# Crossed Horner products for chunks 2 on, shared PSUM banks and a new order, in a delta-rule attention and feed-forward kernel

## The chip, the cores and the metric

The kernel runs on one core of a Trainium2 chip. A core has TensorE (PE in the profile; PEld is its loading of weights), VectorE (DVE), ScalarE (ACT), GpSimd (POOL) and SyncE (SP), which here only issues DMAs. Each engine takes its instructions in the order of its own queue, and semaphores hold one engine until another is done. The metric is the device time of one execution in microseconds.

## The reference

The first part is a linear attention with the delta rule, for 4 batches of 8 heads, 768 positions and head size 48. The keys are normalized per position; `state` is a 48x48 matrix per head.

```python
for t in range(S):
    y[:, :, t] = np.einsum('bhd,bhde->bhe', q[:, :, t], state)
    v_old = np.einsum('bhde,bhd->bhe', state, kt)
    state = state + bt[:, :, :, None] * np.einsum('bhd,bhe->bhde', kt, vt - v_old)
```

The second part takes the 3072 tokens of 384 channels through `w_in` (384x2048), the tanh form of GELU, and `w_out` (2048x384). Inputs and outputs are float32; the kernel computes its matmuls in bf16.

## The kernel before, in words

**Chunks and pairs.** The positions are cut into 12 chunks of 64. The 32 heads make 16 pairs `p`; one head of a pair lies on partitions 0 to 63, the other on 64 to 127 (`HALF`). So an operand of a chunk is a tile of 128 partitions x 16 pairs, and one matmul works on one head with a quarter of TensorE's array.

**Work of a chunk.** `prep` and `prep2` normalize the keys and transpose them (`Kn`, `KQT`), `prepq` does so for the queries of two chunks. `gram` makes the key-key and query-key products, of which ScalarE stores the first (`G`) and VectorE the second, masked (`DT`). `blocks` inverts the triangular 16x16 blocks on the diagonal (`solve`, on GpSimd from chunk 1 on), and `back` transposes the result into `TB0` and `TB1`. `inverse` builds the inverse of the whole 64x64 triangle out of them: it expands the blocks into `WB` and `DI`, multiplies `G` by `WB` and masks it into `ET`, and then runs a Horner scheme over k = 1, 2, 3, in which each step multiplies the last result by `ET` and adds `DI`; the result is `TT`. `state` then makes the residual `R` (values minus what the state recalls), `U` = `TT` times `R`, the next state `S`, and the output of the chunk, which goes into `x`.

**The Horner steps.** Step k makes, for the columns from 16k on, a product of n = 64 - 16k columns (48, 32, 16) for each head: 32 matmuls in PSUM. For chunks 2 on, one VectorE instruction adds the matching columns of `DI` and writes `TT` in bf16. The first step reads `DI`, the others read what the step before has written to `TT`. For chunks 0 and 1 the sum is made in PSUM by matmuls with the identity, and the change does not touch them.

**Placement.** A matmul reads its operands from one half of the partitions and writes to one half of PSUM. In the straight placement, half a writes half a, so that only two of the four quarters of the array are ever used. In the crossed one, the even pairs do this, and the odd pairs write the other half, a ^ (p % 2), in the next bank, so that all four quarters are. Before the change, all of the other products of 32 matmuls of chunks 2 on are crossed (`fl`, in `prod`, `state`); the Horner products are straight. A product that is crossed twice comes out in its own half again, so `DI`, `TT` and `ET` of the odd pairs lie with swapped halves.

**Feed-forward.** `mlp(t)` works on a tile of tokens: chunks 0 to 3 make a tile each, and then two chunks make one. It computes 16 slices of `W1` times `x` in PSUM banks of 512 columns, ScalarE applies the GELU into `gT`, and `W2` times `gT` goes through `osb` to the output. These matmuls use the full array.

**Order.** Nothing is scheduled on the fly. Every operation is recorded by `op` (L101) with its readers and writers; the string `ORDER` (L18) then says which engine takes which operation and in what order, and `BANK` (L78) which PSUM bank each product gets. `w` items are filler matmuls on zeros (`spin`, L411) that keep TensorE busy. `BANKS` (L15) bounds the banks: "t", the attention, had 0 to 5, and "f", the feed-forward, 6 and 7, except for the last tile and early chunks ("l"). `schedule` (L136) gives an operation the waits of its inputs, and, where it takes a bank, those of the bank's earlier users. `load` (L480) issues the DMAs of keys, queries and values on SP, in order: a load behind one that waits for its buffer waits too.

**Lines of the profile.** Operations are recorded by helpers, so all matmuls but the transposes (L648, L680) and the fillers (L414) stand at L267, two-input VectorE and GpSimd operations at L251, copies of VectorE at L256, those of ScalarE at L260. Tile names tell them apart: ps<-DI,ET and ps<-TT,ET are the Horner products, TT<-ps,DI the additions, ps<-WB,G, ps<-R,TT, ps<-U,Kn and ps<-S,KQT crossed products, ps<-x,W and ps<-W,gT the feed-forward (m1 and W,gT below). L924, L931 and L915 expand the blocks.

Of the kernel before, what the change touches and what calls it, by code (L numbers as in the profile page):

```python
# [8 lines left out]
ALU = mybir.AluOpType  # L9
# [5 lines left out]
BANKS = {"t": (0, 6), "f": (6, 8), "l": (0, 8)}  # L15
# [3 lines left out]
v34 a50 g11 s49 v5 v0 g21 v46 a48 s47 g22 v6 g16 v8 v35 v41 g18 s54 v1 v4 a2 g13 g14 s55 g12 g19 v15 v45 s53 a26 v43  # L19
v33 v10 s56 v3 w6.7 p61 v36 v37 v9 v38 s51 v42 v7 v40 s52 a82 g84 v63 s60 a24 g20 v85 g17 a29 v39 v62 a30 a31 v83 a32  # L20
a23 v67 a86 s59 v70 a87 v64 v88 s57 a97 g75 v89 v65 g81 s58 w12.5 p91 v66 a98 p99 g90 v44 v92 g77 w1.4 p93 a103 v68
p100 v94 g72 g76 a101 s96 p152 v104 g74 v153 g73 a105 w1.7 p181 a106 a182 v107 v154 g108 v156 v155 g69 w8.3 p109 v157
v158 v159 a110 v160 v183 g80 s141 a102 v161 w4.5 p264 v162 v163 v164 p178 v265 a179 v165 g266 v166 a117 v167 v168 v169
v170 a25 a28 g267 a27 v171 g268 g269 v172 g270 g271 v173 g272 g273 v174 g274 g275 v175 g276 g277 v176 a185 g278 g279
s95 a184 v177 w29.3 p191 g280 p301 g281 v192 g282 a187 p189 v186 g283 v190 g284 a188 w1.5 p195 g285 v118 p193 g286
a196 g287 a194 p199 v71 g288 v180 p197 g289 a200 g78 a119 p203 v198 a120 g290 a205 p201 v121 g291 v204 v122 g79 a202
p209 a302 p206 g292 g293 s147 v207 a210 g294 g295 a125 v208 s140 v211 g296 w3.5 p215 v303 p216 g297 p217 s146 p304
v218 a219 p212 p123 v126 a305 g299 v298 a127 a128 v129 a133 v306 g130 v300 s115 v124 a213 s113 g400 w12.7 p131 v308
a309 s116 p398 v132 a311 s114 g603 v214 p399 a250 s111 p314 v401 a310 s112 a315 v251 s144 g402 s142 a375 v307 s143
g403 g404 w10.6 p312 v376 a135 s145 g405 p224 g406 s262 g407 p226 v377 a225 g408 v378 s263 v379 p328 a134 g409 v380  # L30
p228 v381 g410 v382 a313 s151 g411 v329 p136 g412 p137 s150 a229 g413 v383 p316 v138 p318 g414 s149 a317 v384 g415
p438 a227 v385 s223 p230 g416 v386 v139 a439 g417 s222 p232 a231 v387 g418 s148 v388 p320 a233 g419 v389 p459 v319
g390 s220 p234 a460 v440 s221 p322 a235 v321 p456 v461 p324 g420 a323 s396 a457 g393 p326 p441 s397 v327 a519 p236
v325 v458 p333 a442 g421 v520 p238 g422 a334 p391 g423 a253 v443 g424 p330 g425 a239 v331 p338 g426 p394 a252 v332
g427 v335 p339 v392 p340 g428 p341 a578 s259 p342 g429 p240 g430 v344 s260 g431 a343 g433 v579 a395 s258 p254 a237
g432 v580 p601 s345 v437 p602 s261 a444 v434 p241 s346 v462 s347 v604 p255 s348 a242 p349 s436 v256 g605 p351 a350
s435 v581 p644 v582 a352 p466 s531 v583 g521 p353 v584 a645 v585 s532 v445 p245 g522 a354 v646 a257 g606 v586 v587
g607 p355 g608 v464 a467 g609 p336 v588 v446 p448 g610 v337 p246 g611 a449 g612 v589 g613 v463 p523 g614 v590 a356
v591 p474 g615 v592 a247 p450 g690 a447 p357 v451 p359 v475 g593 p524 a360 p452 v525 a358 p468 g616 v453 a526 s599
p361 g596 v469 s600 p454 a362 p363 s527 v455 g617 v691 p476 s530 g618 p470 a477 g619 p480 s529 p594 g620 a364 p481  # L40
s528 g621 p478 a482 g622 p365 v479 s483 g623 a771 g624 s489 v471 p366 g625 s491 a595 v772 g626 s488 g627 g628 p533
a243 v773 s490 p662 v774 g629 p597 a244 v775 s492 g630 v776 p370 g631 a598 v777 s487 v778 g632 v779 g633 v780 s703
a367 g634 p371 v781 g636 v782 a692 s702 v783 v784 v785 g635 p794 v534 a372 a663 p795 v640 g786 a465 p493 v647 p495
v664 a494 g693 p472 v797 a496 p497 s792 g883 p499 v473 a498 s793 v637 p535 v648 s638 g796 p501 a536 v884 s699 p539
a502 p540 p641 g798 s486 v541 p694 a642 s639 p503 a500 v643 s700 g799 p695 a504 g800 p505 v696 g801 s548 p507 a506
s546 v697 p537 a665 s547 p651 g789 p659 v652 p509 s701 a508 s550 v538 a660 g802 p790 s549 g803 a374 p510 v661 g804
s698 a958 g805 v791 s551 g806 a249 v649 p837 g807 p669 v959 s484 p653 a248 g808 s485 p514 g809 a838 v654 g810 a668
g811 v670 a511 p515 g812 g813 v667 v839 g814 p552 g815 v960 a516 v961 p655 g816 v962 a553 p834 g817 v656 p677 a835
g818 p554 v963 g819 a650 v678 p556 g820 a555 g821 p657 v836 a557 g822 p558 v658 a886 g823 v666 g824 p679 g825 a559
p683 p671 g826 a680 g827 p560 g828 v672 p681 a561 p562 v682 g829 p673 a563 v830 p684 p704 v674 s832 a685 p564 v705  # L50
s545 p675 a565 s831 p852 v676 a369 p566 v964 s542 a853 v965 p710 v966 s544 p706 v967 a567 p568 v968 s543 v969 a707
v970 v841 a368 v854 p711 p855 v971 a712 p569 v860 v972 v859 g973 a856 v833 s719 p787 a373 v842 s720 p573 v857 a858
g885 s717 s721 p974 v840 a517 s722 p708 v788 p862 a570 g976 p574 s718 v863 a512 s688 v709 s687 g981 p864 a575 p977
s689 a576 v865 p887 s686 g1133 p888 v975 p723 v889 p844 a724 p725 v845 a861 p727 a843 v978 a726 p979 v890 a728 p980
p846 v982 p729 p731 v847 g983 a730 p1019 a732 p866 p1022 g984 v867 p848 g985 a1023 g986 p733 v849 g987 p735 g988 v1024
g989 p1131 a736 g990 g991 p1132 a734 g992 a1020 p737 g993 v1021 p739 g994 a738 g995 v1134 p870 a740 g996 p741 g997
p743 v871 a742 g998 g999 p850 a518 g1000 p868 a744 g1001 p745 v869 g1002 v851 p747 g1003 a746 g1004 p872 a748 p876
g1005 p749 a873 g1006 g1007 p751 a750 g1008 p874 g1009 a752 p877 g1010 v875 p753 a878 g1011 g1012 p1037 g1013 p891
a754 p755 v892 a577 g1135 a513 v1015 p897 a571 p893 s1016 g1014 p756 v894 a1038 s716 s715 g1136 v1018 g1137 p898 p1040
s714 g1138 a899 p759 g1139 s1017 v757 g1140 a1041 g1141 v1039 s713 p760 g1142 a572 v1043 s907 g1143 a1025 v1042 g1144  # L60
s906 p763 g1145 v1044 s904 v1026 g1146 a758 s908 g1147 v1045 v761 p1171 g1148 s905 p1029 a1172 p764 g1149 s909 a1028
g1150 v1173 s903 g1151 v1030 p767 g1152 a765 s881 g1153 v1027 s879 g1154 p1047 s882 g1155 p895 p1031 g1156 s902 p910
g1157 v1032 s880 g1158 p768 a911 g1159 v1048 g1160 g1161 p912 v896 g1162 g1163 p1174 g1164 a913 p1049 g1165 p1033 a769
v1050 a1175 p914 g1166 v1034 p916 a915 p1055 v1170 a917 p1051 p918 v1052 p920 v1177 a919 v1056 p1035 a921 p1053 a762
# [233 lines left out]
def bass_deltanet__then__act_gelu_tanh_kernel(  # L298
# [25 lines left out]
    with nc.allow_non_contiguous_dma("head rows"), nc.allow_low_precision("bf16 matmuls"):  # L324
# [568 lines left out]
        def inverse(c, hs):  # L893
# [5 lines left out]
            def nm(t, g):  # L899
                return [f"{t}_{y}" for y in ((g,) if c < 2 else (0, 1))]  # L900
# [439 lines left out]
```

## Time and profile before

| | us |
|---|---|
| runs | 252.25, 252.91, 249.76 (median 252.25) |
| profiled execution, span from first to last instruction | 249.4 |
| end of its last matmul | 246.5 |
| TensorE busy | 232.0 (93%) |
| VectorE busy | 161.4 (65%) |
| ScalarE busy | 139.0 (56%) |
| GpSimd busy | 118.6 (48%) |
| mean granted TensorE clock | 0.986 of full |
| 10 additions of 768 columns, mean | 0.945 |
| 10 of 512 columns | 0.686 |
| 10 of 256 columns | 0.421 |

The profiled execution's own time is not listed apart from the runs; its span is 0.4 us under the fastest of them and 2.85 us under the median. The busy time of an engine says little by itself, since the stages differ: up to about 43 us the chunk-0 chain runs through VectorE and TensorE is kept busy with fillers; from 50 us on TensorE has real work nearly always. The prediction therefore reads stages.

### The profile page before, as it was taken

What the parts mean: (1) busy time and instruction counts of PE and PEld (TensorE: products, weight loads), DVE (VectorE), ACT (ScalarE), POOL (GpSimd) and SP (SyncE); (2) the same over time, 40 slices, a digit from 0 to 9 for tenths busy, and PEclk for the clock granted to TensorE, in tenths of its full rate; (3) what the DMA queues carried; (4) which work ended last, traced back from release to release, by engine and by line L of the source; (5) the groups of instructions that cost most, each with busy time, mean ns of one, the idle gap of its engine ahead of it and who ended that gap; (6) DMA issues with size and microseconds to landing.
All of it is one profiled execution on the core that took longest, in us unless ns stands there. A gap on an engine that the chain in (4) does not pass through costs nothing.

```text
span 249.4 us, 12386 instructions
## 1 busy us (share of the span) xinstructions
PE 232.0 (93%) x5637; PEld 155.0 (62%) x5637; DVE 161.4 (65%) x316; ACT 139.0 (56%) x262; POOL 118.6 (48%) x249
## 2 busy tenths in 40 slices
PE   7577896998999799999899999999999999999995
PEld 4334473587778658868766655666656665555562
DVE  6699989886799399896969653767772465100001
ACT  2744578587686466838564357535682247426600
POOL 3685796688389858588045589883000000000000
PEclk9999999799999799999999999999999999999999
DMA  6999969996740825550244000623135210000112
GB/s 157 209 196 168 159 116 211 159 214 107 184 87 19 192 52 112 122 137 7 57 111 91 5 20 23 149 57 63 37 76 134 78 37 3 8 11 32 66 63 96
DMA packets 64789, 23.84 MB, mean 96 GB/s; under 512 B 53600, under 2 KB 63840, under 8 KB 64736
## 3 DMA queue, kind: packets, MB, share of 16 engines
q1 hardware_dynamic: 58656, 14.89, 30.8%
q0 software_dynamic: 1056, 3.15, 7.3%
q10 hardware_dynamic: 5024, 5.02, 6.3%
q8 instruction: 44, 0.72, 1.2%
q14 instruction: 9, 0.07, 0.1%
HBM read 20.64 MB, written 4.72 MB: 102 GB/s over the span
## 4 chain that ended last, share of the span: by engine, by line
PE 81%; DVE 10%; DMA 2%; issue 2%; ACT 2%; POOL 0%; ACTq 0%; POOLq 0%
PE ps L267 76%; DMA kf<-in_k_dram 2%; PE ps L648 2%; PE ps L680 2%; PE ps L414 1%; DVE ss L603 1%; DVE WB L931 1%; ACT WB L915 1%; DVE TB L806 1%; DVE KQT L256 1%; DVE ps L846 1%; DVE Yf L251 1%; DVE Tt L837 1%; DVE btz L251 0%; DVE ps L786 0%
## 5 line engine op out<-in xcount | busy, mean ns | idle before, releaser
L260 ACT ACTIVATE gT<-ps 128x512 bf16<-128x512 f32 x96 | 55.9, 597 | 38.4 <-PE ps L267 36.8
L267 PE MATMUL ps<-x,W 128*128 128x256 bf16 (+1 forms) x384 | 72.2, 329 | 0.0
L267 PE MATMUL ps<-W,gT 128*128 128x384 bf16 x384 | 67.0, 328 | 0.0
L267 PEld LDWEIGHTS ps<-W,gT 128*128 128x128 bf16 x384 | 36.4, 98 | 23.9 <-issue 0.5
L267 PEld LDWEIGHTS ps<-x,W 128*128 128x128 bf16 x384 | 39.1, 115 | 16.3 <-issue 0.3
L762 POOL TENSOR_TENSOR Yf<-Yf,tmp 128x28 f32<-128x28 f32 (+13 forms) x84 | 28.8, 342 | 6.4
L759 POOL TENSOR_TENSOR tmp<-Yf 128x28 f32<-128x28 f32 (+13 forms) x84 | 28.1, 335 | 6.1
L251 DVE TENSOR_TENSOR TT<-ps,DI 128x768 bf16<-128x768 f32 (+2 forms) x30 | 20.2, 684 | 13.8 <-PE ps L267 13.5
L414 PE MATMUL ps<-wz 128*128 128x512 bf16 x87 | 23.3, 416 | 1.4 <-DVE wz L409 1.4
L251 POOL TENSOR_TENSOR Kn<-kf,rn 128x768 bf16<-128x768 f32 (+1 forms) x11 | 16.0, 1452 | 17.1 <-DVE rn L629 10.1
L267 PE MATMUL ps<-KQT 48*32 48x32 bf16 (+1 forms) x1152 | 18.7, 195 | 5.8 <-issue 2.7
L260 ACT ACTIVATE osb<-ps 128x384 f32<-128x384 f32 x18 | 8.8, 490 | 26.3 <-PE ps L267 26.3
L256 DVE COPY osb<-ps 128x384 f32<-128x384 f32 x6 | 3.2, 552 | 29.8 <-PE ps L267 29.8
L260 ACT ACTIVATE G<-ps 128x512 bf16<-128x512 f32 x24 | 14.3, 597 | 11.4 <-PE ps L267 7.7
L267 PEld LDWEIGHTS ps<-KQT 48*32 48x32 bf16 (+1 forms) x1152 | 13.6, 95 | 10.9 <-issue 5.0
L719 DVE TENSOR_TENSOR DT<-ps,mD 128x512 bf16<-128x512 f32 x24 | 16.3, 680 | 4.1 <-ACT G L260 4.1
L267 PE MATMUL ps<-TT,ET 64*64 64x32 bf16 (+1 forms) x768 | 16.4, 176 | 0.0
L267 PEld LDWEIGHTS ps<-TT,ET 64*64 64x64 bf16 x768 | 14.8, 109 | 2.2 <-DVE R L251 0.6
L414 PEld LDWEIGHTS ps<-wz 128*128 128x128 bf16 x87 | 8.7, 105 | 11.5 <-issue 3.0
L251 DVE TENSOR_TENSOR S<-ps,S 128x768 bf16<-128x768 f32 x10 | 9.5, 953 | 9.0 <-PE ps L267 8.9
L260 ACT ACTIVATE x<-ps 128x1024 bf16<-128x1024 f32 (+2 forms) x10 | 9.2, 916 | 8.1 <-PE ps L267 7.9
L251 DVE TENSOR_TENSOR R<-ps,vf 128x768 bf16<-128x768 f32 x11 | 10.4, 949 | 3.8 <-PE ps L267 3.8
(122 smaller groups left out, 333.2 us busy)
## 6 DMA issues: line engine op xcount, KB each, us to landing
qf<-in_q_dram SPq DMA_DIRECT2D x24, 192.0 KB, 4.4
kf<-in_k_dram SPq DMA_DIRECT2D x23, 192.0 KB, 4.9
vf<-in_v_dram SPq DMA_DIRECT2D x40, 96.0 KB, 3.2
out_dram<-osb ACTq DMA_DIRECT2D x16, 192.0 KB, 2.0
W<-in_moe_w_out_dram POOLq DMA_DIRECT2D x4, 384.0 KB, 6.7
out_dram<-osb ACTq DMA_DIRECT2D x16, 96.0 KB, 2.8
W<-in_moe_w_in_dram POOLq DMA_DIRECT2D x4, 192.0 KB, 8.7
vf<-in_v_dram SPq DMA_DIRECT2D x4, 192.0 KB, 11.3
```

The lines of the kernel that those rows point to most:

```text
L251: return lambda e: e.tensor_tensor(out() if callable(out) else out, a() if callable(a) else a, b() if callable(b) else b, op)
L256: return lambda e: e.tensor_copy(out, a() if callable(a) else a)
L260: return lambda e: e.activation(out, a() if callable(a) else a, func)
L267: ins = t.matmul(out, lhsT, rhs, start=st, stop=sp_, skip_group_check=skip)
L414: ins = e.matmul(psum[:, b, :], wz[:, 0:128], wz[:, :], start=True, stop=True)
L603: op({"dve": 0.95 * w}, {"dve": lambda e, u=u: e.tensor_reduce(ss[j][:, u], sq[:, u, :], AX.X, ALU.add)}, reads=[f"sq{n}"], writes=[f"ss{j ...
L648: ins = e.transpose(o[:, a, j], Qn[:, n, a, j, :, :].rearrange("q h d -> q (h d)"), identB[:, :])
L680: ins = e.transpose(tb()[:, m, :], t[:, 2 * m:2 * m + 2, :].rearrange("p h d -> p (h d)"), identB[:, :])
L719: op(d_ps(512), {"dve": lambda e: e.tensor_tensor(dv, gview(1)(), md, ALU.mult)}, reads=[h] + MD, writes=[dn])
L759: sop(nb * s * w, lambda e, s=s, w=w, tv=tv: e.tensor_tensor(tv, yf[:, :, s:s + 1, 0:s].to_broadcast([128, nb, w, s]), Yv()[:, :, s + 1:16 ...
L762: sop(nb * s * w, lambda e, s=s, tv=tv: e.tensor_tensor(Yv()[:, :, s + 1:16, 0:s], Yv()[:, :, s + 1:16, 0:s], tv, ALU.add), [YN, TN], [YN])
L806: op({"dve": 0.58}, {"dve": lambda e: e.transpose(dst, src)}, reads=reads, writes=writes)
```

## The change

It has three parts. The Horner products of chunks 2 on are crossed: odd pairs write the other half of PSUM, in the second of two banks, and the addition, which has to bring them back to the half they belong to, becomes three VectorE instructions, one for the even pairs over all partitions and one for each half of the odd pairs. The bounds of the banks fall: all work may use all eight. And `ORDER` and `BANK` are new. Two operands of the product's record change with it: the bank class is "t", and the product takes two banks at every k.

In the new order the loads of the first keys, queries and chunk 0's values come as before; behind them the order differs. Fifty operations change their engine, most of them between VectorE and ScalarE: for instance the expansions of `WB` in chunk 1 go to ScalarE, and the `ET` products of chunk 1 to VectorE. VectorE's queue goes from 307 operations to 302, ScalarE's from 268 to 276, GpSimd's from 238 to 235, and TensorE has 88 fillers for 87. GpSimd issues the weights' loads in the same order. On SP, two of the four quarters of chunk 2's values now stand behind chunk 7's keys.

```diff
-BANKS = {"t": (0, 6), "f": (6, 8), "l": (0, 8)}
+BANKS = {"t": (0, 8), "f": (0, 8), "l": (0, 8)}
...
-                    op({"pe": 0.467 * w}, bk="l" if c < 2 else "t", fns={"pe": prod(hk, ET[e_], src[:, :, 16 * k - off:64 - off], n, per, g)},
-                       nm=int(32 * w), reads=nm(sn, y) + nm(f"ET{e_}", y) + ([f"DI{r_}e"] if fl else []), free=nm(f"TT{r_}b", y),
-                       writes=[hk], alloc=[(hk, max(1, int(NP * w) // per))])
-                    op(d_ps(16 * n * w), {"dve": f_tt(two(TT[r_][:, :, cols], per, g), view(hk, n, per, g),
-                                                      two(DI[r_][:, :, 16 * k - 16:48], per, g), ALU.add)},
+                    def place(p, hk=hk, n=n):
+                        return bank(hk, p % 2)[:, n * (p // 2):n * (p // 2) + n]
+
+                    def cross(src=src, off=off, k=k, place=place):
+                        return [(place(p)[HALF[a ^ (p % 2)], :], ET[e_][HALF[a], p, :], src[HALF[a], p, 16 * k - off:64 - off],
+                                 True, True, True) for p in range(NP) for a in range(2)]
+
+                    def add(e, hk=hk, n=n, k=k, cols=cols):
+                        for par, o_, i_ in ((0, slice(0, 128), slice(0, 128)), (1, HALF[0], HALF[1]), (1, HALF[1], HALF[0])):
+                            ins = e.tensor_tensor(TT[r_][o_, par::2, cols],
+                                                  bank(hk, par)[i_, 0:8 * n].rearrange("q (p t) -> q p t", t=n),
+                                                  DI[r_][o_, par::2, 16 * k - 16:48], ALU.add)
+                        return ins
+                    op({"pe": 0.274}, {"pe": f_mms(cross)}, bk="t", nm=32,
+                       reads=nm(sn, y) + nm(f"ET{e_}", y) + ([f"DI{r_}e"] if fl else []), free=nm(f"TT{r_}b", y),
+                       writes=[hk], alloc=[(hk, 2)])
+                    op({"dve": 3 * (0.10 + 1.06e-3 * 8 * n)}, {"dve": add},
                        reads=[hk] + nm(f"DI{r_}", y) + ([f"DI{r_}e"] if fl else []), writes=nm(f"TT{r_}b", y))
```

The lists of `ORDER` and `BANK` (about 1300 entries) are left out.

## The prediction

> **What bounds the kernel now.** I read the page's first two parts, the chain that ended last, a table by stages, and TensorE's timeline, in that order.
>
> The page: busy time of each engine, then the 40 slices.
>
> ```profile
> PE 232.0 (93%) x5637; PEld 155.0 (62%) x5637; DVE 161.4 (65%) x316; ACT 139.0 (56%) x262; POOL 118.6 (48%) x249
> ...
> PE   7577896998999799999899999999999999999995
> ...
> DVE  6699989886799399896969653767772465100001
> ...
> PE 81%; DVE 10%; DMA 2%; issue 2%; ACT 2%; POOL 0%; ACTq 0%; POOLq 0%
> ```
>
> TensorE is full from slice 8 (50 us) on, and the chain is 81% TensorE. VectorE is the second engine, and it is crowded only up to slice 33 (206 us); after that only the feed-forward part runs. In the chain in order of time, three pieces show where TensorE takes over:
>
> ```profile
> 39.90 2.58 DVE WB L931 x3
> ...
> 44.35 3.42 PE ps L414 x10
> ...
> 144.07 102.42 PE ps L267 x2080
> ```
>
> Up to 43 us the chain runs through VectorE; ten filler matmuls (L414) follow; the last 102 us are one unbroken stretch of matmuls. So past 50 us a microsecond of matmul is a microsecond of time, as long as the other engines keep up. The stage table shows how far they do (columns: stretch, length, then busy us of PE, PEld, DVE, ACT, POOL, then clock and DMA):
>
> ```profile
> 36.00:50.10 14.10, 12.00 (x304) 7.40 (x297) 12.82 (x26) 10.30 (x22) 9.38 (x16) 0.88 0.93 182
> 50.10:130.40 80.30, 77.01 (x2312) 61.05 (x2313) 64.78 (x128) 53.94 (x97) 54.09 (x104) 0.98 0.51 108
> 130.40:246.50 116.10, 115.42 (x2560) 70.74 (x2546) 53.46 (x77) 55.02 (x97) 30.62 (x69) 1.00 0.20 53
> ```
>
> I cut the stages where the first product of chunk 1's state ends (50.1 us) and where chunk 5's last state product ends (130.4 us). In the middle stage VectorE works 64.8 of 80.3 us, 15.5 us of slack; in the last, 53.5 of 116.1.
>
> **The product itself.** The edit turns the 30 Horner products of chunks 2 to 11 (10 chunks, k = 1, 2, 3) from the straight to the crossed placement. The other 64x64 products of these chunks are crossed already, so the timeline has both, 32 matmuls each (start, us, then what ran):
>
> ```profile
> 156.19 0.43 PE L267 MATMUL ps<-R,TT 64*64 64x48 bf16 x32
> 156.56 1.47 PE L267 MATMUL ps<-W,gT 128*128 128x384 bf16 x8
> ...
> 166.14 0.42 PE L267 MATMUL ps<-U,Kn 64*64 64x48 bf16 x32
> 166.40 0.69 PE L267 MATMUL ps<-DI,ET 64*64 64x48 bf16 x32
> 167.01 0.84 PE L267 MATMUL ps<-x,W 128*128 128x512 bf16 x3
> ...
> 169.98 0.66 PE L267 MATMUL ps<-DI,ET 64*64 64x48 bf16 x32
> 170.48 0.66 PE L267 MATMUL ps<-TT,ET 64*64 64x32 bf16 x32
> 171.07 1.49 PE L267 MATMUL ps<-x,W 128*128 128x512 bf16 x6
> ```
>
> From start to start, ahead of a full-array matmul: straight 0.61 (166.40 to 167.01), crossed 0.37 (156.19 to 156.56). Ahead of another 64x64 product: straight 0.50 (169.98 to 170.48), crossed 0.26 (166.14 to 166.40). The column count hardly matters (TT,ET of 32 columns is as long as DI,ET of 48). The difference is 0.24 either way. I take 0.21, since some neighbours shorten it by a few hundredths: 30 x 0.21 = **6.3 us less TensorE work**, bounds 5.4 (0.18) and 7.2 (0.24). The Trainium skill, "TensorEngine Tiling (Array Packing)", Theoretical Speedup, puts the gain of packing a small dimension at up to two times, which on the straight 0.50 to 0.61 would be 0.25 to 0.30 a product, 7.5 to 9 us; the rows say 0.24 and decide.
>
> **The additions.** Each of the 30 additions was one VectorE instruction; it becomes three (even pairs on 128 partitions, odd pairs as two half-height ones that cross the halves), each over half the columns. Rows by form: TT<-ps,DI of 768, 512 and 256 columns takes 945, 686 and 421 ns, 2.05 us a chunk. For the new sizes, 384 columns is ET<-ps,mE at 550, 256 is 421, 128 is the cast at 287. A half-height row costs what its columns say (bpad<-ps 64x192 takes 354), so height saves nothing. Three of each, with some 0.06 overlap between neighbours as in the timeline: 1.53 + 1.15 + 0.74 = 3.42 a chunk, 1.37 more; over ten chunks **+13.7 us on VectorE**. The strided write and the crossing of halves are in no row; bounds 1.0 to 2.0 us a chunk. It hides where TensorE has other work queued; where it has none, the next product waits for it, since k = 2 needs the sum of k = 1.
>
> **The new order** moves work too, and I counted it stage by stage. Between chunk 1's residual and chunk 5's state on VectorE it holds the twelve additions of chunks 2 to 5 (+5.5 us), two more ET products (+1.9) and two more long x copies for a short one (+1.8), and it loses KQT copies and a block expansion to ScalarE or to other stages (about -2.1): 64.8 + 7.1 = **72 us**. TensorE between the same two products loses 12 x 0.21 = 2.5 to the edit, and one m1 group (0.66), two W,gT groups (2.6) and two transposes (0.9) to other stages; two fillers come in (0.4). 77.0 - 6.3 = **71 us**, plus the 3.3 us in which it now idles there, 74. So the engines are level where VectorE had 15.5 us of slack. ScalarE gets eight operations more, some 5 us at the 597 ns of its commonest row, against 54 of 80 busy. All eight banks open to all work takes away waits for a bank; k = 2 and 3 now take two banks instead of one. No wait on a bank stands alone in the list of waits, so I set both at nothing, within 1 us either way.
>
> **Loads.** SP's queue is in order. In the new one two quarters of chunk 2's values stand behind chunk 7's keys, which wait until chunk 4's keys are read (Kn at 54.7 to 56.2 us now), and the second of them also behind a load of queries, the like of which is issued at 62.0 now. They land some 3.2 us after issue, by 66, and chunk 2's residual is due near 78: hidden by 12 us; beyond that, every microsecond counts. POOL's queue issues the same weight loads in nearly the old order. POOL's solves keep their rows; chunk 1's two XW products change places there, which brings the first 1.2 us later, to about 37.5, when VectorE comes to it near 38 anyway.
>
> **The start.** The DMA of chunk 0's keys and the chunk-0 chain stay. Then WB of chunk 1, the 2.58 us piece at 39.90, moves to ScalarE, where its three parts take 389 ns each, and chunk 3's transposed keys no longer stand behind it. Against that, two copies of chunk 0's factors (0.5 and 0.4) come onto VectorE, and chunk 0's x copy falls behind a table load (1.28 us). I take 1.5 us earlier into the middle stage; bounds 1 us later and 3 us earlier.
>
> **The end.** The last two copies to osb both fall on ScalarE, with output DMAs between them: +0.3 us.
>
> **The sum.** Middle stage: two engines with 74 and 72 us that feed each other with queues in order do not overlap perfectly; VectorE in its fullest stretch now (100 to 125 us) reaches 20.65 of 25, 83%. I take 77 (bounds 74, and 87.5 below): -3.3. Last stage: 3.8 us of feed-forward and transposes moved in, 18 x 0.21 = 3.8 out: level. Start -1.5, end +0.3: together -4.5. The profiled execution's span is 249.4, so 244.9. Its own time is not listed; the median of the runs shown, 252.25, lies 2.85 above the span, so **247.8 us** (-1.8%). The runs before differ by 1.2% among themselves; 2% is about what a measurement here can tell from no change.
>
> **Rivals.**
>
> 1. *VectorE is hidden.* The order interleaves feed-forward matmuls with nearly every Horner step, so TensorE might never wait. Middle stage 74 (-6.3), start -2, end +0.3: 241.4, a time of 244.2. For it: VectorE has no total overload. Against it: 72 of 74.
> 2. *VectorE becomes the bound and keeps its idle time.* Its 15.5 us of idle in the middle stage are mostly waits for a product ("TT <- ps" alone sums to 13.5 us over the run). The chain of one chunk (product, three instructions, product) gets longer, and S of chunk c gates R of chunk c+1. If all of it stays, the stage is 72 + 15.5 = 87.5 (+7.2); start level, end +0.3: 256.9, a time of 259.8, **slower**. It decides as soon as the stage passes 80.3 + 4.8, that is, if more than 13 us of the idle time stay; with less the time is within 2%. Against it: part of that idle came from TensorE being late, and TensorE has 6 us less to do. The Trainium skill, "TensorEngine Tiling (Array Packing)", PSUM Bottleneck, says that the copy out of PSUM may become the bottleneck once the array is packed, and asks for copies vectorized over tiles of a bank; the edit splits one instruction into three. By that rule this rival or the forecast holds, not the first.
> 3. *The crossed Horner products do not overlap* (each quarter waits for its sum): nothing off TensorE, additions still paid. Middle stage about 79.5, last +3.8, start -1.5, end +0.3: 251.2, a time of 254. WB,G and R,TT, crossed with the same shapes, speak against it.
>
> **Chances.** Forecast 0.37, VectorE hidden 0.28, VectorE bound 0.27, no overlap 0.05, something else 0.03. The forecast's own range is 245 to 251, a third of it under 247.2 (2% faster). Over all cases: faster by 2% 0.37 x 0.3 + 0.26 = 0.37 and a little; same 0.25 of the forecast, 0.08 of the second rival, 0.07 of the rest; slower mostly the second rival. I say 0.38, 0.40, 0.22. The range reaches from 1.7 under the first rival's time, for the upper bound of the product's gain, to most of the way to the second's: 242.5 to 256.
>
> **What would show it.** In the profile after: the products ps<-TT,ET and ps<-DI,ET of 32 should stand 0.26 to 0.37 from the next start; if 0.5, the third rival. TT<-ps,DI should appear as 90 rows with means near 550, 421 and 290 ns; means over 700 for the largest would make VectorE the bound. VectorE's busy share before chunk 5's state should pass 85%, and waits of PE or PEld for "TT L..." should grow from the 2.2 us they have now. If those waits stay under 2 us, the first rival holds; over 8 us, the second. The forecast is also wrong if TensorE's clock falls in new gaps (0.88 in the stage before 50 us now), or if the loads come late.

## The result and the profile after

The kernel after takes 249.76 us, the median of 20 runs (246.31 to 252.41, and one that stands alone at 525.61). The kernel before, in 20 runs beside it, takes 251.71 us (249.76 to 254.56). The ratio is 0.986, with an interval from 0.983 to 0.989: about 3.5 us faster. Ratios here leave out runs more than 1.5% above the fastest of their own kernel; the medians of all runs differ by less, 1.95 us or 0.8%. The profiled execution took 250.40 us, with a span of 248.6, and so lies in the upper half of its kernel; a second profile of the same kernel (after_again, below) has a span of 245.7.

The page after: busy time of each engine, the slices of TensorE and VectorE, the granted clock, and the chain that ended last.

```profile
PE 229.0 (92%) x5638; PEld 150.3 (60%) x5638; DVE 172.8 (69%) x368; ACT 139.7 (56%) x267; POOL 113.7 (46%) x246
...
PE   7587899999899898799999999999999999999995
...
DVE  6689957986878799799999576789887755100000
...
PEclk9999957999999999999999999999999999999999
...
PE 61%; DVE 24%; DMA 5%; SPq 4%; issue 3%; ACT 2%; POOL 0%; DVEq 0%
```

TensorE works 3.0 us less (232.0 before), VectorE 11.4 us more. The chain now runs through VectorE for 24% of the span, where it was 10%; in after_again, the same kernel, it is 13%. In the clock row, the sixth and seventh slice (31 to 43 us) stand at 5 and 7 tenths: that is the start of the kernel, and it comes back below.

The table by stages, cut at the same two products as before (stretch, length, busy us of PE, PEld, DVE, ACT, POOL, clock, DMA):

```profile
36.00:50.90 14.90, 14.23 (x350) 9.50 (x346) 12.70 (x25) 11.23 (x25) 9.91 (x17) 0.83 0.78 150
50.90:129.60 78.70, 72.55 (x2303) 55.65 (x2307) 68.49 (x150) 54.63 (x99) 50.26 (x101) 1.00 0.52 114
129.60:245.70 116.10, 114.69 (x2560) 68.80 (x2553) 63.69 (x116) 55.48 (x100) 30.09 (x69) 1.00 0.20 52
```

The middle stage begins 0.8 us later than before (50.9 against 50.1), is 1.6 us shorter (78.7 against 80.3), and the last stage is the same to 0.1 us. In the middle stage TensorE has 4.5 us less to do and idles 6.2 us where it idled 3.3. VectorE is busy 87% of that stage.

TensorE's timeline shows the products that were changed (start, us, what ran):

```profile
166.00 0.44 PE L266 MATMUL ps<-DI,ET 64*64 64x48 bf16 x32
166.28 0.40 PE L266 MATMUL ps<-KQT 48*64 48x128 bf16 x16
...
169.56 0.43 PE L266 MATMUL ps<-TT,ET 64*64 64x32 bf16 x32
169.83 0.42 PE L266 MATMUL ps<-DI,ET 64*64 64x48 bf16 x32
170.18 2.13 PE L266 MATMUL ps<-x,W 128*128 128x512 bf16 x9
```

From start to start they take 0.28, 0.27 and 0.35 us, where the straight ones took 0.50 and 0.61. The additions by form (busy us and mean ns of one, idle time of VectorE before them):

```profile
L1020 DVE TENSOR_TENSOR TT<-ps,DI 64x384 bf16<-64x384 f32 x20 | 11.1, 555 | 0.3
...
L1020 DVE TENSOR_TENSOR TT<-ps,DI 64x256 bf16<-64x256 f32 x20 | 8.4, 422 | 0.3
...
L1020 DVE TENSOR_TENSOR TT<-ps,DI 64x128 bf16<-64x128 f32 x20 | 5.8, 288 | 0.3
...
L1020 DVE TENSOR_TENSOR TT<-ps,DI 128x384 bf16<-128x384 f32 x10 | 5.5, 549 | 0.4 <-PE ps L266 0.2
```

Half the partitions cost as much as all of them (555 against 549 ns), and neither the strided write nor the crossing of halves costs more than 5 ns over what a row of 384 columns without them took before (ET<-ps,mE, 550 ns).

### The profile page after: what moved, and what is told of

The parts are those of the page before. It is cut to its first block, busy times and chain, and to the rows that moved or that the text cites. A ratio compares the mean times of both kernels' runs of the same rounds, so it can differ in the third digit from the quotient of the medians.

```text
span 248.6 us, 12457 instructions
## 1 busy us (share of the span) xinstructions
PE 229.0 (92%) x5638; PEld 150.3 (60%) x5638; DVE 172.8 (69%) x368; ACT 139.7 (56%) x267; POOL 113.7 (46%) x246
## 4 chain that ended last, share of the span: by engine, by line
PE 61%; DVE 24%; DMA 5%; SPq 4%; issue 3%; ACT 2%; POOL 0%; DVEq 0%
PE ps L266 55%; DVE TT L1020 6%; SPq L274 4%; PE ps L413 3%; DMA kf<-in_k_dram 2%; PE ps L647 2%; DVE ss L602 2%; DVE R L250 1%; DVE DT L718 1%; DMA x<-x 1%; DMA vf<-in_v_dram 1%; PE ps L679 1%; DVE TB L805 1%; DVE ET L250 1%; DVE KQT L255 1%
## 5 line engine op out<-in xcount | busy, mean ns | idle before, releaser
L259 ACT ACTIVATE gT<-ps 128x512 bf16<-128x512 f32 x96 | 53.3, 601 | 28.3 <-PE ps L266 27.6
L1020 DVE TENSOR_TENSOR TT<-ps,DI 64x384 bf16<-64x384 f32 (+5 forms) x90 | 37.9, 421 | 8.5 <-PE ps L266 7.5
L761 POOL TENSOR_TENSOR Yf<-Yf,tmp 128x72 f32<-128x72 f32 (+13 forms) x84 | 28.6, 341 | 5.7
L758 POOL TENSOR_TENSOR tmp<-Yf 128x112 f32<-128x112 f32 (+13 forms) x84 | 28.0, 335 | 5.8
L413 PE MATMUL ps<-wz 128*128 128x512 bf16 x88 | 24.3, 424 | 1.3 <-DVE pat L420 1.3
L250 POOL TENSOR_TENSOR Kn<-kf,rn 128x768 bf16<-128x768 f32 (+1 forms) x11 | 15.9, 1451 | 17.4 <-DVE rn L628 15.2
L259 ACT ACTIVATE KQT<-ps 128x1024 bf16<-128x1024 bf16 x11 | 11.1, 1021 | 8.0 <-PE ps L679 4.1
L250 POOL TENSOR_TENSOR Yf<-Tt,bM 128x512 f32<-128x512 f32 x5 | 6.4, 1283 | 18.2 <-DVE Tt L874 8.7
L266 PEld LDWEIGHTS ps<-TT,ET 64*64 64x64 bf16 x768 | 10.9, 112 | 5.0 <-issue 2.8
L602 DVE TENSOR_REDUCE ss<-sq 128x16 f32<-128x768 f32 (+1 forms) x13 | 11.5, 881 | 2.9 <-POOL sq L250 2.4
L266 PE MATMUL ps<-TT,ET 64*64 64x32 bf16 (+1 forms) x768 | 12.6, 180 | 0.5 <-DVE TT L1020 0.5
```

Source lines behind the costliest of these rows:

```text
L250: return lambda e: e.tensor_tensor(out() if callable(out) else out, a() if callable(a) else a, b() if callable(b) else b, op)
L259: return lambda e: e.activation(out, a() if callable(a) else a, func)
L266: ins = t.matmul(out, lhsT, rhs, start=st, stop=sp_, skip_group_check=skip)
L413: ins = e.matmul(psum[:, b, :], wz[:, 0:128], wz[:, :], start=True, stop=True)
L602: op({"dve": 0.95 * w}, {"dve": lambda e, u=u: e.tensor_reduce(ss[j][:, u], sq[:, u, :], AX.X, ALU.add)}, reads=[f"sq{n}"], writes=[f"ss{j ...
L758: sop(nb * s * w, lambda e, s=s, w=w, tv=tv: e.tensor_tensor(tv, yf[:, :, s:s + 1, 0:s].to_broadcast([128, nb, w, s]), Yv()[:, :, s + 1:16 ...
```

## The experiments

All ratios are against the kernel before, with 95% intervals; 1% is 2.5 us. The stage tables of the experiments have the columns of the one above.

### The product edit and the order, apart

**straight_new_order** keeps the new order and the new banks and undoes the product edit.

```diff
-                    op({"pe": 0.274}, {"pe": f_mms(cross)}, bk="t", nm=32,
+                    op({"pe": 0.467 * w}, ..., fns={"pe": prod(hk, ET[e_], src[:, :, 16 * k - off:64 - off], n, 8, g)},
...
-                    op({"dve": 3 * (0.10 + 1.06e-3 * 8 * n)}, {"dve": add},
+                    op(d_ps(16 * n * w), {"dve": f_tt(two(TT[r_][:, :, cols], 8, g), view(hk, n, 8, g), ..., ALU.add)},
```

> The kernel after with its order, its banks and its two banks per product, but the Horner products straight and each addition one VectorE instruction again. Theory (the gain is TensorE time in the last stage, and the middle stage is shared by two engines): 30 x 0.21 = 6.3 us of TensorE come back, some 17 us of additions leave VectorE; the middle stage stays near 78.7 us because TensorE, with 75 us of work, takes the place of VectorE there, and the last stage grows by 18 x 0.21 = 3.8 us. So 3 to 4.5 us above the kernel after, a ratio of 0.998 to 1.006 against the kernel before. Rival (the new order brings the gain and the crossing nothing): 0.986, as the kernel after. Third (the crossing costs more on VectorE than it saves): below 0.983.

Measured: 1.001 (0.996 to 1.005). The new order alone is worth nothing, as the theory had it; the crossing, on top of it, is worth 0.986 against 1.001, that is 3.6 us, with 1.4 either way (against after_again, on the same chip, 4.5 with 2.2).

```profile
50.21:129.31 79.10, 73.95 (x2285) 57.95 (x2286) 61.60 (x124) 55.56 (x103) 50.71 (x103) 1.00 0.53 114
129.31:248.12 118.81, 118.69 (x2584) 73.14 (x2570) 53.55 (x81) 55.39 (x100) 30.05 (x69) 1.00 0.20 51
```

In the last stage TensorE is full to 0.1 us, and the crossing shortens it from 118.8 to 116.1 or 115.3. In the middle stage 79.1 stands against 78.7 and 78.2.

**crossed_old_order** does the reverse: the order of before with the product edit. All banks are open to all, and 8 of the 276 bank numbers change.

> The kernel before with its order, but the Horner products crossed and each addition three instructions; all eight banks open, and 8 of the 276 bank numbers changed so that the products of k = 2 and 3 get two banks. Theory: the last stage loses 3.8 us as TensorE has all of that stage to itself; in the middle stage TensorE loses 2.5 us and VectorE gains 8 (12 additions by the rows of the kernel after), 64.8 + 8 = 73 of 80: level, 79 to 82 us. Ratio 0.982 to 0.992. Rival (without the new order VectorE's longer additions hold TensorE up, and the order is what makes the crossing pay): middle stage 84 to 87, ratio 1.000 to 1.012.

Measured: 1.033 (1.028 to 1.039), a median of 259.59 us. The theory missed, and the rival's price was too low. The same edit that gains 3.6 us in the new order loses 8.3 in the old one. The stages, and the first line of TensorE's list of waits (us in total, times, longest):

```profile
50.72:135.77 85.05, 76.78 (x2316) 59.25 (x2317) 70.70 (x152) 53.99 (x97) 53.87 (x103) 0.96 0.49 102
135.77:256.97 121.20, 113.03 (x2556) 66.93 (x2544) 64.84 (x113) 55.15 (x97) 30.59 (x69) 1.00 0.20 51
```

```profile
PE ps L267 <- DVE TT L1021: 7.9, 10, 1.4
```

Even the last stage, where VectorE works only 65 of 121 us, is 5 us longer than before; the loss is not VectorE's total. The timeline shows what it is:

```profile
83.17 0.42 PE L267 MATMUL ps<-TT,ET 64*64 64x16 bf16 x32 [0.58 <-DVE TT L1021]
83.53 0.85 PE L267 MATMUL ps<-x,W 128*128 128x256 bf16 x6
85.83 0.44 PE L267 MATMUL ps<-R,TT 64*64 64x48 bf16 x32 [1.45 <-DVE TT L1021]
```

The old order puts one short group of feed-forward matmuls (0.85 us) between a Horner product and the next product that needs its sum. That was enough for one VectorE instruction; for three it isn't, and everything behind the waiting product in TensorE's queue waits too. In the trace of before, the closest of the thirty products that read a fresh sum starts 0.24 us after it was written; here nine start within 0.06 us of it. Seven of the ten waits, 5.1 us, stand in front of such a product. The other three, 2.8 us, stand in front of a state product (ps<-S,KQT), which reads no sum; that it waited for the bank which the addition was still reading is likely and not shown. Part of this profile's middle stage is a half clock: two stretches of 3.4 us that follow such waits; its execution took 261.63 us, 2 us more than the median.

**one_add_old_order** is the same with the addition as one instruction, which tells the additions from the crossing and the banks.

```diff
-                        for par, o_, i_ in ((0, slice(0, 128), slice(0, 128)), (1, HALF[0], HALF[1]), (1, HALF[1], HALF[0])):
-                            ins = e.tensor_tensor(TT[r_][o_, par::2, cols], ...
+                        return e.tensor_tensor(TT[r_][:, :, cols].rearrange("q (p b) t -> q b p t", b=2),
+                                               psum[:, b0:b0 + 2, 0:8 * n].rearrange("q b (p t) -> q b p t", t=n),
+                                               DI[r_][:, :, 16 * k - 16:48].rearrange("q (p b) t -> q b p t", b=2), ALU.add)
```

> The kernel of crossed_old_order (old order, crossed Horner products, 8 bank numbers changed), but the addition is one VectorE instruction as before the change; it leaves out bringing the odd pairs back to their half, so that part of the result is not computed. Theory (in the old order the longer additions hold TensorE up, since the next Horner product stands right behind): the 8 us that crossed_old_order lost come back and the products' saving shows: middle stage 78 to 79, last stage 112.5 to 113, ratio 0.972 to 0.985. Rival (the crossed products themselves, or the changed banks, cost the time in the old order): near crossed_old_order, above 1.02.

Measured: 0.993 (0.989 to 0.997). The 8.3 us come back, so the additions caused them. But the gain is 1.8 us, not the 3.8 to 7 that were expected:

```profile
50.64:130.73 80.09, 74.07 (x2319) 57.78 (x2318) 64.85 (x129) 53.96 (x97) 54.98 (x105) 1.00 0.51 108
130.73:244.65 113.92, 111.88 (x2548) 66.58 (x2536) 53.54 (x77) 55.02 (x97) 30.48 (x69) 1.00 0.21 54
```

TensorE works 2.9 and 3.5 us less than before in the two stages. Some 1.4 of the first is a half clock that before had there, and this execution had not: one run of the same matmuls takes 5.48 us in before (from 84.28) and 4.12 here (from 83.75). But TensorE idles 6.0 instead of 3.3 us and 2.0 instead of 0.7. In the middle stage the new idle time is a wait of 1.1 us for a DMA of `x`, 0.9 for VectorE (TT and R), and 0.8 more without a releaser. So in this execution a part of what the shorter matmuls saved turned into waiting.

### Are the additions hidden in the new order?

**one_add** is the kernel after with the same single instruction.

> The kernel after, but the addition is one VectorE instruction over both banks and all partitions; it leaves out bringing the odd pairs back to their half, so that part of the result is not computed. TensorE has the same work in the same order, VectorE some 17 us less. Theory (in the middle stage VectorE holds TensorE up): TensorE's idle time there falls from 6.2 us to the 3.3 us of the kernel before, the stage from 78.7 to 75.5 to 76, the last stage by 0 to 0.5: 3 to 3.5 us under the kernel after, ratio 0.971 to 0.977. Rival (VectorE is hidden and the idle time has other causes): as the kernel after, 0.984 to 0.988.

Measured: 0.990 (0.985 to 0.995), beside **after_again**, the kernel after unchanged on the same chip:

> The kernel after, unchanged, on the same chip as the three others: ratio 0.983 to 0.990. Its profile is to tell whether the granted clock of one half from 31 to 41 us belongs to the kernel (then it is there again, and the middle stage begins at 50.5 to 51 us) or to that one execution (then the stage begins near 48.5 to 49.5 us, as was forecast). The middle stage 78 to 79.5 us, the last 115.5 to 116.5.

at 0.983 (0.975 to 0.990). With 18.9 us less work than in the first profile of after, VectorE makes the kernel no faster: the theory falls, the rival holds. First one_add, then after_again:

```profile
49.99:128.73 78.74, 72.34 (x2291) 55.77 (x2295) 61.54 (x125) 55.58 (x103) 50.83 (x103) 1.00 0.53 116
128.73:243.92 115.19, 114.50 (x2560) 68.79 (x2560) 53.04 (x80) 55.35 (x100) 30.06 (x69) 1.00 0.20 52
```

```profile
49.21:127.44 78.23, 72.32 (x2285) 55.33 (x2286) 68.13 (x148) 55.58 (x103) 50.84 (x103) 1.00 0.53 116
127.44:242.74 115.30, 114.67 (x2584) 68.86 (x2572) 63.97 (x117) 55.39 (x100) 30.10 (x69) 1.00 0.20 53
```

VectorE is 6.6 us lighter in the middle stage of one_add, and TensorE's idle time is 6.4 against 5.9 us. after_again's profile also answers its own question: its half clock between 28 and 42 us lasts 3.4 us instead of 10.2, and its middle stage begins at 49.2, so the slow start differs between executions of one kernel. The middle stage of the new order is not held up by the length of the additions, although VectorE is 87% busy there and although the chain that ended last goes through it. In the whole first profile of after, TensorE waits for their sums twice (total, times, longest):

```profile
PE ps L266 <- DVE TT L1020: 0.6, 2, 0.5
```

The chain of that profile:

```profile
104.72 0.96 DVE ET L250
105.68 1.09 DVE DI L923
106.77 1.20 DVE DT L718 x2
...
125.83 2.28 DVE x L255 x2
...
198.50 47.21 PE ps L266 x585
```

Such a chain says which work ended last at each step, not how much later anything would be if that work were longer or shorter; from 110 to 130 us TensorE was busy 19.8 of 20 us beside it.

How far the cover reaches was measured with longer additions. **add_split2** cuts each of the three instructions into two, **add_split4** into four, over as many columns in all.

```diff
+                            for z in range(4):
+                                sl = slice(4 * z + par, 4 * z + 4, 2)
+                                ins = e.tensor_tensor(TT[r_][o_, sl, cols], ...
```

> The kernel after, with each of the three VectorE instructions of an addition cut into two, each over half the pairs. The rows of the kernel after (550, 422 and 288 ns for 384, 256 and 128 columns) lie on a line of 1.03 ns a column and 157 ns an instruction, so an addition gets 3 x 0.157 = 0.47 us longer and VectorE 14 us busier, nearly as much again as the change added. TensorE has the same work. Theory (the new order keeps only 0 to 2 us between a sum and the next product, and seven of thirty steps have under 0.3): the steps with too little cover pass on 2 to 2.5 us, ratio 0.988 to 1.000. Rival (VectorE is hidden with room to spare, as one_add suggests): as the kernel after, 0.981 to 0.987.

Measured: 0.990 (0.981 to 0.999). This is inconclusive. The ratio rests on two of twelve runs; the median of all twelve, 252.96, lies 0.6% above that of before, where the kernel after lies 0.8% under it.

> The same with each instruction cut into four: an addition gets 9 x 0.157 = 1.4 us longer, VectorE 42 us busier, 214 us in all. Summing what each step would lack by the slack in the profile of after_again gives 14 to 15 us: ratio 1.03 to 1.05. If even this is hidden, below 1.0; then only VectorE's total counts.

Measured: 1.042 (1.036 to 1.048), as the slack step by step had it. Its list of waits of TensorE, and its stages:

```profile
PE ps L266 <- DVE TT L1022: 9.4, 14, 1.7
```

```profile
49.20:133.86 84.66, 72.65 (x2282) 55.43 (x2285) 74.82 (x256) 55.17 (x100) 50.25 (x101) 1.00 0.49 105
133.86:258.65 124.79, 117.60 (x2587) 69.34 (x2575) 74.86 (x279) 55.44 (x100) 30.22 (x69) 0.99 0.19 49
```

So the additions are hidden in the new order, but the room ends soon behind them. 1.4 us more for each of thirty would be 42 us; 14 of them come through, in the last stage too, where VectorE has 50 us of idle time. What counts is the time between a sum and the product that needs it: nine of the 14 waits, 5.7 us, stand in front of such a product, and the others in front of matmuls that read no sum, as with the state products above. In the trace of after_again it is under 0.3 us in nine of thirty steps (the expectation of add_split2 has seven) and 1 us or more in fifteen.

### Where the crossing pays

**straight_2_to_5** takes the crossing back in chunks 2 to 5, **straight_6_to_11** in chunks 6 to 11, by a condition on `c` ahead of the two forms shown above.

> The kernel after, with the Horner products of chunks 2 to 5 straight and their additions one instruction, those of chunks 6 to 11 as in the kernel after. The prediction's price for these twelve products was 2.5 us of TensorE. Theory now (in the middle stage the crossing saves next to nothing, since TensorE, made faster, only waits longer for its next instructions and for the chain of a chunk): middle stage 78.7 to 79.3 and last stage 115.2 to 116.2, 0 to 1 us above the kernel after, ratio 0.983 to 0.990. Rival (the prediction's price): 2.5 us above, 0.992 to 0.998.

Measured: 0.991 (0.987 to 0.995).

> The counterpart: chunks 2 to 5 as in the kernel after, chunks 6 to 11 straight with one instruction. Theory now: middle stage 78.2 to 78.8, last stage 118.5 to 119.5, 3 to 3.5 us above the kernel after: ratio 0.995 to 1.003, as straight_new_order. Rival (the middle stage's twelve products bring their 2.5 us): 0.988 to 0.992.

Measured: 1.001 (0.998 to 1.004). Four kernels of one order now differ only in which products are crossed, and with them in the additions:

| crossed | ratio |
|---|---|
| none | 1.001 (0.996 to 1.005) |
| chunks 2 to 5 | 1.001 (0.998 to 1.004) |
| chunks 6 to 11 | 0.991 (0.987 to 0.995) |
| all (20 runs) | 0.986 (0.983 to 0.989) |

The medians of all runs keep this order: 1.009, 1.002, 0.995 and 0.992 of the median of before.

Chunks 6 to 11 bring 2.4 us, with 1.5 either way (first row to third), or 3.8 with 1.1 (second to fourth); 18 x 0.21 = 3.8 was forecast. Chunks 2 to 5 bring -0.1 with 1.4, or 1.2 with 1.2; together some 0.6 with 0.9, where 12 x 0.21 = 2.5 was forecast.

The profiles say the same after one correction. The middle stage of these executions, first straight_2_to_5, then straight_6_to_11:

```profile
50.21:131.13 80.92, 74.05 (x2283) 58.17 (x2286) 61.09 (x124) 55.59 (x103) 50.87 (x103) 1.00 0.52 112
```

```profile
51.06:126.36 75.30, 71.73 (x2283) 55.28 (x2285) 68.25 (x148) 54.54 (x99) 50.25 (x101) 1.00 0.53 116
```

75.3 us against 78.7 and 78.2 in the two profiles of after: up to the end of this stage these three executions have the same instructions in the same order. The waits of TensorE within it tell what differs, in the first profile of after and in straight_6_to_11:

```profile
PE ps L266 <- issue: 3.2, 4, 1.4
PE ps L647 <- issue: 1.0, 1, 1.0
```

```profile
PE ps L266 <- issue: 0.7, 1, 0.7
```

"issue" is idle time for which the profile shows no releaser. Less these gaps, counting those of 0.25 us or more, and leaving out profiles with a half clock in the stage, it takes 74.5, 75.5, 74.6, 74.6 and 75.3 us where chunks 2 to 5 are crossed (after, after_again, straight_6_to_11, one_add, fill_again), and 76.2 and 76.0 where they are straight (straight_new_order, straight_2_to_5): 1.2 us for twelve products. What these gaps are is told in the last section.

The products themselves do save their price here. Summed over the stage, from the start of each Horner product to the start of the next matmul and without idle time, they take 8.7 and 8.8 us in the two straight profiles and 5.8 to 6.0 in the five crossed ones: 2.6 to 3.0 us less. More than half of that comes back in other matmuls, which stand a little further apart, and in short waits.

### The start

**fill_start** adds five filler matmuls where TensorE idles in chunk 0's inverse; **fill_again** is the same kernel a second time.

```diff
-p189 g279 v186 g280 a187 v190 p191 ... s141 p199
+w2.7 p189 g279 v186 g280 a187 v190 w1.7 p191 ... s141 w2.7 p199
```

> The kernel after with five more filler matmuls where TensorE waits in chunk 0's inverse: two before the first product with WB (behind the 29 fillers there), one before the second, two before the Horner product of k = 2. Five at 0.216 are 1.1 us of filler in 1.6 us of idle time. Theory (the granted clock of one half from some 31 to 39 us in the profiles of the new order follows that idle time, and slows chunk 0's real products): the clock stays at one there, the middle stage begins at 48 to 49 us, 0.5 to 1.5 us under the kernel after: ratio 0.977 to 0.982. Rival: the fillers push the chain of chunk 0 back by as much, or the clock falls anyway: 0.983 to 0.990.

> The kernel of fill_start a second time. There the middle stage began at 48.2 us, as expected, but a half clock of 3.4 us fell twice into the middle stage of that profile. If that was chance, the ratio is now 0.977 to 0.983; if the fillers only shift the slow clock to later, again 0.985 to 0.993.

Measured: 0.990 (0.983 to 0.996) and 0.985 (0.980 to 0.990). The stretch from 28 to 42 us, first in after, then in fill_again (the last three columns are the clock, the share of DMA and GB/s):

```profile
28.00:42.00 14.00, 12.20 (x287) 9.14 (x287) 10.60 (x24) 10.23 (x27) 11.00 (x28) 0.63 0.76 128
```

```profile
28.00:42.00 14.00, 11.62 (x387) 8.13 (x390) 11.71 (x26) 11.52 (x30) 12.56 (x29) 1.00 0.77 137
```

In both profiles of the filled kernel the clock there is 1.00, and the middle stage begins at 48.2 and 48.4 us instead of 50.9 and 49.2. That looks like the theory, but is not shown to be the fillers' work. The clock rows of add_split2, which has no fillers, of fill_again, and of straight_2_to_5_fill, which has them:

```profile
PEclk9889999999999999799999999999999999999999
```

```profile
PEclk9999999999999999999999999999999999999999
```

```profile
PEclk9889999997999999999999999999999999999999
```

The clock between 28 and 42 us is 1.00 in three of the eight profiles of the new order without fillers too (add_split2, add_split4, straight_2_to_5). Their middle stages begin at 49.2 to 50.2 us, and that of straight_2_to_5_fill at 49.8; all four have a half clock of 3.4 us that begins between 10.9 and 13.0 us, ahead of the first filler added (after 27 us). The two profiles that begin at 48.2 and 48.4 have no half clock ahead of the stage at all. So the early half clock seems to cost as well, and chance may have a part in the earlier start. And no gain in time is left that these runs could tell: one ratio lies above those of the kernel after, 0.986 and 0.983, and the other between them. In fill_start's profile, at 253.67 us one of its two longest runs, two half-clock stretches of 3.4 us lay in the middle stage; in fill_again's, at 246.12, there was none anywhere. Whether the fillers move the low clock to later or chance did so isn't settled.

**straight_2_to_5_fill** puts both together:

> straight_2_to_5 with the five fillers of fill_start. With straight products TensorE has less idle time in the middle stage, so that the clock should fall there more seldom; with the fillers the clock stays up at the start. If both hold, 0.5 to 1 us under straight_2_to_5: 0.978 to 0.987. If the fillers bring nothing, as straight_2_to_5.

Measured: 0.995 (0.991 to 0.999), not better than straight_2_to_5. Its profile has a half clock from 58.9 to 62.3 us, in the middle stage: straight products did not keep the clock up there in this execution. No variant beat the kernel after by more than the intervals hold.

## Why the prediction was right

The forecast was 247.8 us within 242.5 to 256, a gain of 1.8%; the median is 249.76 and the gain 1.4% by the ratio, 0.8% by the medians. The sign and the range were right, and the size nearly. How the time comes about was right for the last stage and wrong for the middle one, where errors partly cancelled. By its steps:

**The product.** Right: 0.27 to 0.35 us from start to start, some 0.24 less than straight ones. The third rival, no overlap, is out. TensorE's busy time against straight_new_order fell by 4.0 us in the last stage, as 18 such products should make it, but by 1.4 in the middle one, where the twelve save their price too and more than half of it comes back around them.

**The additions.** The rows were right to 5 ns (549 to 555, 422 and 288 against 550, 421 and 287 taken), but +13.7 us was too little: 37.9 against 20.5 us of additions is +17.4, and VectorE's total in the same order went from 155.3 to 172.8. The mis-sized term is the 0.06 us of overlap between neighbours: I subtracted it for each neighbour, though nine additions in a row in the timeline of after (from 170.06) take 3.94 us, the full 3.79 of their rows and a little more.

**The middle stage.** Here the size was nearly right by luck, and the reason wrong. I put 77 us, as two engines of 74 and 72 us that do not overlap perfectly. Executions with this code and without a half clock took 78.7, 78.2, 75.3 and 76.9. But one_add, with 61.5 us of VectorE instead of 68.5, took 78.7 too: the lost overlap with VectorE, 3 us in my sum, isn't there. In its place stand 0.7 to 4.2 us in which TensorE waited for nothing that the profile shows. TensorE's work came out at 71.7 to 72.6 us in the profiles of this code above, where I had 71. The 77.0 us that I started from held one half-clock stretch of 3.4 us, which made the matmuls some 1.4 us longer; the 0.98 in the clock column of that row said so, and I passed over it. That this error hardly shows in the sum is luck as well: the edit and the moved work took off 3 to 4 us and not the 6.3 that I subtracted.

**"Past 50 us a microsecond of matmul is a microsecond of time."** This premise holds for the last stage (18 products: 2.4 to 3.8 us of 3.8) and fails for the middle one (12 products: about 1 of 2.5, although from start to start they save 2.6 to 3.0).

**The first rival**, VectorE hidden, names the mechanism that the runs show in the new order. Its price of 244.2 us was too low for the reasons just given, and for the start.

**The second rival**, that VectorE's latency becomes the bound, is close to what the edit does in the old order. That 259.59 us were measured there and 259.8 forecast for the new order is a coincidence: the rival put all of the loss into the middle stage, and the profile has half of it in the last one. By the Trainium skill ("TensorEngine Tiling (Array Packing)", PSUM Bottleneck), which I set beside this rival, the copy out of PSUM may become the bottleneck after a fourfold speedup of TensorE. Here the products took about half of their time, and the old order's 7.9 us of waits for TT agree with it, the new order's 0.6 do not. So the chance of 0.27 was not idle; which of the two came true was decided by the distance in TensorE's queue between a product and the reader of its sum, and I had counted work by engine and stage, not that distance.

**What would show it.** TensorE's waits for the sums were 0.6 us on PE and 2.8 on PEld in the first profile, 1.9 on PEld in the second: at the threshold of 2 that I had set for the first rival. VectorE's share passed 85% as foretold, and meant nothing: 87% with three instructions and 78% with one took the same time.

**Loads.** Right for chunk 2: in the whole trace one R waited for values, 0.8 us at 194 us, for chunk 10, not 2.

**The start.** Forecast -1.5; measured +0.8 and -0.9. What I left out is the clock. After ran at half clock from 30.8 to 41.0 us and after_again in three stretches of 3.4 us (from 11.6, 21.8 and 35.5); before had one, from 43.3. Without any ahead of the stage it began 1.7 and 1.9 us earlier than before (both with fillers). Since before itself had a half clock there, how much of that the order brings is not shown. I had named a fall of the clock in new gaps as a danger, but not priced it.

**The end** came out at nothing (2.9 us from the last matmul to the end of the span in both) instead of +0.3, and the last stage level, as forecast.

**The step from span to time** was mis-sized by 1.05 us: I added 2.85, the distance from the profiled span to the median of three runs. Profiled executions with both numbers lie 1.8 us apart (250.40 and 248.6). The profiled execution of before was thus itself a run of about 251.2, a microsecond under the median that I used. With 1.8 the forecast would have been 246.7, 3 us under the measured median instead of 2: this error hid a third of the others.

## What to carry to other kernels

A product made cheaper at the price of a longer evacuation (the work that takes the result out of PSUM) pays only if the order gives the evacuation room. The same edit cost 8.3 us in one order and brought 3.6 in another that alone was worth nothing, so count, for each product, the work queued between it and the first reader of its result. A busy share of 87% and a chain through an engine do not show that the engine holds up another; taking its work away, or adding to it, tells.

## What the runs showed of the hardware

**Unexplained gaps of TensorE end shortly after a block of instructions lands.** The packets on queue q8, of kind "instruction", are 44 blocks of 16384 bytes in each profile; TensorE has 5638 matmuls and as many weight loads, which makes 256 of them to a block. In the middle stages of the 14 profiles there are 58 idle gaps of TensorE of 0.25 us or more that have no other releaser. Each of them ends 1.2 to 1.7 us after such a block has landed, though blocks come some 4.5 us apart there. In no profile do two blocks start less than 3.27 us apart. For the two kernels (gap's end, its length, time since the last block landed, us):

```
before   57.96 0.72 1.70    66.36 0.33 1.35    84.28 1.26 1.71   123.78 0.75 1.48
after    68.03 0.99 1.51    72.30 0.57 1.72    86.24 0.79 1.37    98.59 0.42 1.39   103.33 1.38 1.35
```

This looks as if stretches of small matmuls used up their instructions faster than new ones come. That a crossed product, which spends its 64 instructions in 0.27 us instead of 0.5, gains less in such a stretch would fit, but no run changed the number of instructions alone, so the cause of the gaps and this link are argued and not shown. The gaps sum to 0.7 to 5.0 us in a middle stage and differ between executions of the same instructions, 4.2 and 2.8 us in the two profiles of after. The Trainium skill ("Runtime: NRT & Kernel Launch", Instruction fetch mechanics) has the blocks of 16 KiB and 256 instructions, which agrees, and calls the cost of crossing them mostly hidden; if the gaps here are that cost, they do not bear it out.

**The clock falls in steps.** But for those that the end of a profile cuts off, every stretch of half clock in the 14 profiles lasts 3.41, 6.83 or 10.24 us, and within one profile they begin whole multiples of 3.41 us apart. Between one and two microseconds of idle time in the 3.41 us ahead can be enough: 1.2 us in before ahead of 84.21, 1.2 us in after ahead of 30.75 (half clock up to 40.99), 1.9 us in crossed_old_order ahead of both of its stretches in the middle stage. They are not always: the 1.9 us of idle time in the same length ahead of 12.53 us in before were followed by none. The Trainium skill ("TensorE: Matmul & The Clock Gate", Part 1) tells of a free-running activity window of some 3.4 us; the 3.41 agrees.
